# An mLSTM cell and a squared-ReLU FFN on one core: output gates by Tanh, and another order around chunk 2

## Chip, cores, metric

The kernel runs on one core of one Trainium2 chip. The metric is the device time of one execution in microseconds (us); where several executions are given, their median counts. A profile is of one execution. TensorE (PE), VectorE (DVE), ScalarE (ACT), GpSimd (POOL) and SyncE (SP, which here only issues DMAs) each work off their own instructions in the order of the program; semaphores hold an instruction until what it needs is there.

## What is computed

There are 4 batches, 8 heads, 768 steps and a head dimension of 40. The attention part is a recurrence with exponential gates; its output is gated, joined over the heads to rows of 320 and sent through a squared-ReLU feed-forward network (FFN) of width 2048. Everything is float32, and the weights come as float64, as word pairs.

```python
m_new = max(f_gate[t] + m, i_gate[t])
f_stab, i_stab = exp(f_gate[t] + m - m_new), exp(i_gate[t] - m_new)
C = f_stab * C + i_stab * outer(v[t], k[t])
n = f_stab * n + i_stab * k[t]
denom = max(abs(n @ q[t]), 1.0)
o = 1.0 / (1.0 + exp(-o_gate[t]))
y[t] = o * (C @ q[t]) / denom
...
x = y as rows of (batch, step), 320 wide           # 3072 rows
out = max(x @ w_in, 0.0) ** 2 @ w_out
```

## The kernel before

**Tiling.** The 3072 rows are 24 chunks of 128 steps (`NT`), six to a batch; two chunks make a group of the FFN (`GT`). Within a chunk the recurrence is a masked product: `transposes` turns keys and queries, `scores(s)` multiplies them on TensorE (L535), `weigh(s)` makes the decay weights W with exponentials on ScalarE (L464, L468; `mask` on GpSimd at L422 comes first), `weighted(s)` multiplies scores and W on VectorE to P (L549), and `attend(s)` forms three products: `hi` from the state C carried over (L558), `dC` for the new state (L565) and `hp` from P (L572). GpSimd updates the state (L586, L591). `normalise(s)` (from L730) divides by the clipped denominator, multiplies by the output gate `og` and makes the row tile x; `turn_rows(s)` turns it by TensorE (L774) and ScalarE copies it into xT (L775), the input of the first FFN products `ffn1(g, pp)` (L796, L807). Their results go through `relu_half` (L820) and `square_half` (L826) on ScalarE. From chunk 6 (`X_SQ`) on, `normalise_turned` (from L708) takes the place of `normalise`, and x is turned through memory.

**Weights.** The float64 weights arrive in 18 pieces. For each, `Rounding.words` makes two tiles, mag and low, on ScalarE (L211, L213), and `Rounding.join` puts them together: three VectorE operations (L222, L226, L227) and an add on GpSimd (L231), which also lets the next piece be fetched. `rounding.step()` is one of each, with the words a piece ahead of the join. ffn1(0,0) needs pieces 0 to 2; ffn1(0,1) pieces 3 and 4; ffn1(0,2) pieces 5 to 7; ffn1(0,3) pieces 8 and 9.

**Order.** The order is written out by hand and no scheduler moves it. An opening (L1069 to L1128) runs chunks 0 and 1 and prepares chunk 2; a loop of eight steps u (L1133 to L1185) takes chunks 2 to 5, two steps to a chunk, each with one `ffn1`; the long loop over `parts` (L1213) takes chunks 6 to 23, with the FFN products mixed in. In the long loop the attention work is spread over four places `at` per chunk.

**Buffers that matter here.** PSUM gives attention three banks in turn (`ps_at`): scores take two, and the next `hi`, `dC` and `hp` take the third and then the two of the scores once `weighted` has read them. FFN products take banks of `ps_h`: three in the opening, so the second bank of one `ffn1` is the first of the one before, free when its ReLU has read it.

**Gates.** `load_o` brings the output gates, and `sigmoid(s)` (L381) puts them through ScalarE's Sigmoid, in place, 128x320 a chunk. It is called for chunks 0 and 1 before attend(0), for 2 and 3 in the opening, for 4 to 7 at u = 5, and for four chunks at a time in the long loop (L1273). ScalarE's functions come from tables, and a load (ACT_TABLE_LOAD) stands ahead of the first sigmoid of each place and ahead of the first exponential after it (L464 in the opening and the loop of eight, L445 later). On ScalarE the opening runs, after the exponentials of chunk 1: gates 0 and 1, words of pieces 2 and 3, xT of chunk 0, key and query copies of chunk 2, gates 2 and 3, xT of chunk 1, exponentials of chunk 2, words of pieces 4 and 5, exponentials of chunk 3.

Of the kernel before, what the change touches and what calls it, by code (L numbers as in the profile page):

```python
# [13 lines left out]
AF = mybir.ActivationFunctionType  # L14
ALU = mybir.AluOpType
# [14 lines left out]
def kernel(  # L30
# [27 lines left out]
    nc = tc.nc  # L58
    B, H, S, D = q.shape
# [187 lines left out]
    rounding = Rounding()  # L247
# [37 lines left out]
    st = {}  # L285
# [14 lines left out]
    KQ_SQ, X_SQ, ROT = 7, 6, 8  # L300
# [76 lines left out]
        og = st.setdefault(s, {})["og"] = st["og", r][:, s - s0]  # L377
        nc.sync.dma_start(og, o_gate[b, :, c * P : (c + 1) * P, :].rearrange("h p d -> p h d"))

    def sigmoid(s):  # L380
        nc.scalar.activation(st[s]["og"], st[s]["og"], AF.Sigmoid)  # L381

    def load_A(s):
        b, c = divmod(s, NB)
# [154 lines left out]
    def weighted(s):  # L539
        d = st[s]  # L540
        d["P"] = []
        for i in range(2):
            heads = slice(i, H, 2)
            t = d["W"][:, heads, :] if s < ROT else d["W"][:, i::2, DP:]
            if s < W_IN:
                at = 2 * H * P + W * (2 * (s % 2) + i)
                t = flat_c[:, at : at + W].rearrange("p (j t) -> p j t", j=PR)
            d["P"].append(t)
            nc.vector.tensor_tensor(t, d["sc"][i], d["W"][:, heads, :] if s < ROT else t, op=ALU.mult)  # L549
# [180 lines left out]
    def normalise(s):  # L730
        d = st[s]
        num = d["num"]
        if num is not d["hp"]:
            nc.vector.tensor_tensor(num[:], num[:], d["hp"][:], op=ALU.add)
        dm = work.tile([P, H], F32, name="dm")
        nc.vector.tensor_scalar(dm[:], num[:, :, D], scalar1=-1.0, scalar2=1.0, op0=ALU.mult, op1=ALU.max)
        nc.vector.tensor_tensor(dm[:], dm[:], num[:, :, D], op=ALU.max)
        nc.vector.reciprocal(dm[:], dm[:])

        x = d["x"] = work.tile([P, 3 * P], F32, name="x_sb")  # L740
        x3 = x[:, :DM].rearrange("p (h d) -> p h d", d=D)
        nc.vector.tensor_tensor(x3, num[:, :, :D], d["og"], op=ALU.mult)
        nc.vector.tensor_tensor(x3, x3, dm[:].unsqueeze(2).to_broadcast([P, H, D]), op=ALU.mult)
        nc.vector.tensor_copy(x[:, DM:], x[:, DM - KR : DM])

# [23 lines left out]
    def turn_rows(s):  # L769
        d = st[s]  # L770
        t = xT_half(s)
        tp = ps_at.tile([P, 3, P], F32, name="tp", tag="at")
        for a in range(3):
            nc.tensor.transpose(tp[:, a, :], d["x"][:, a * P : (a + 1) * P], ident[:])  # L774
        nc.scalar.copy(t, tp[:])  # L775
        del st[s]
# [329 lines left out]
    load_A(2)  # L1106
    load_o(2)
    load_o(3)
    sigmoid(0)
    sigmoid(1)  # L1110
    attend(0)
    rounding.step()
    normalise(0)
# [7 lines left out]
    idle(4)  # L1121
    transposes(2)
    idle(4)
    sigmoid(2)
    sigmoid(3)
    turn_rows(1)
    weigh(2, masked=True)
    rounding.step()  # L1128


# [2 lines left out]
    for u in range(8):  # L1133
        s = 2 + u // 2
        relu_half()
        if u % 2 == 0:
            if u == 0:
                ffn1(0, 0)
                scores(s)
                rounding.step()  # L1140
            else:
                turn_rows(s - 1)
                scores(s)
                ffn1(u // 4, u % 4)
            if u == 2:
                rounding.words()
            weighted(s)
            if u == 2:
                mask(s + 1)
                rounding.join()  # L1150
                rounding.join()
                weigh(s + 1, masked=True)
                rounding.words()
            else:
                weigh(s + 1)
                square_half()
        else:
            load_A(s + 2)
            for r in {1: (4,), 3: (5, 6), 5: (7,), 7: ()}[u]:
                load(r)  # L1160
            if u == 5:
                for r in range(4, 8):
                    sigmoid(r)
            attend(s)
            if u == 3:
                square_half()
            rounding.join()
            normalise(s)
            for r in {5: (8,), 7: (9,)}.get(u, ()):
                load(r)  # L1170
            for r in {5: (7,), 7: (8,)}.get(u, ()):
                pair_up(r)
            if u > 4:
                load_o(2 * s)
                load_o(2 * s + 1)
            transposes(s + 1)
            rounding.words()
            ffn1(u // 4, u % 4)
            square_half()
        if u < 4:  # L1180
            load_o(4 + u)
        while rounding.done < NEXT[u]:
            rounding.step()
        if u in WIN_SUMS:
            sums_of_win(WIN_SUMS[u])  # L1185
# [27 lines left out]
    for n, (which, g, i) in enumerate(parts):  # L1213
        s, at = 6 + n // 4, n % 4
        if n == 5:
            brought.close()
            late = ctx.enter_context(tc.tile_pool(name="late", bufs=1, side="right"))
        even = s >= 8 and s % 2 == 0
        fast = which == 1
        if at == 0:  # L1220
            if s < 8 or even:
                do(scores, s)
            if even:
                do(turn_kq, s + 1)
            if s < 8 or even:
                do(weighted, s)
        if at == 1:
            do(attend_begin, s)
            if even:
                do(lambda s: scores(s, ("h", "h")), s + 1)  # L1230
            if fast:
                ffn1_rows(g, 0, True)
            do(attend_end, s)
            do(decays, s + 1)
            do(mask, s + 1)
            if n > 4 and not even and not fast:
                do(turn_kq, s + 1)
            do(decay_C, s + 1)
            if s > X_SQ and not fast and not even:
                do(turn_squares, s - 1)  # L1240
            do(store_num, s)
            do(load_num, s)
            do(load_squares, s + 2)
            if even:
                do(load_A, s + 2)
        if 5 <= n < 8:
            sums_of_weights(n - 5)
        if n == 6:
            sums(1, slice(0, NPAIR), (1, 2))
        if n == 8:  # L1250
            sums_of_weights(3)
            sums(1, slice(0, NPAIR), (3,))
        if n == 9:
            sums(1, slice(0, NPAIR), (4,))
        if which == 2 and i == 3 and g == NG - 2:
            sums(g + 1, slice(0, NPAIR), (2,))
        if which == 2 and g > 1 and i < 2:
            sums(g, slice(0, NPAIR), (3 + i,))
        if n == 0:
            ffn1_begin(g)  # L1260
            sums_of_x(g)
            sums_of_win(2)
        if at == 3 and s >= 8 and s % 2 == 0 and s // 2 - 1 < NG:
            sums_of_x(s // 2 - 1)
        if at == 2 and not fast:
            if even:
                do(turn_squares, s - 1)
            if n > 4:
                do(scale_q, s + 1)
        if at == 3:  # L1270
            if s % 4 == 3:
                for r in range(s + 1, min(s + 5, NT)):
                    sigmoid(r)  # L1273
        if fast:
            if i % 2:
                ffn1_close(g, i // 2, i == 1)
                if at == 1 and g > 2:
                    do(turn_kq, s + 1)
                    do(turn_squares, s - 1)
            else:  # L1280
                ffn1_open(g, i // 2)
                if i == 0 and g > 2:
                    sums(g - 1, slice(0, NPAIR), (2,))
            if at == 2 and g > 2:
                do(scale_q, s + 1)
        elif g == 0:
            ffn2(g, *divmod(i, 2))
        else:
            ffn2_fast(g, i)
        if at == 2:  # L1290
            do(lambda s: weigh(s, masked=True), s + 1)
            ffn1_square()
            if n < 4:
                do(turn_kq, s + 1)
                do(scale_q, s + 1)
            if even:
                do(weighted, s + 1)
            do(normalise_turned, s)
            do(store_rows, s)
            if not even:  # L1300
                do(load_A, s + 2)
            if s > 6:
                do(load_o, s + 5)
            do(load_rows, s)
            if s == 6:
                do(pair_up, s + 3)
        if s > 6 and at == (3 if even else 2):
            do(pair_up, s + 3)
        if s > 6 and at == 3:
            if s == 7:  # L1310
                load(s + 3)
            do(load, s + 4)
        if n in (9, 25):
            spread_slots(2 + n // 25)
        if at == 0:
            ffn1_square()
        if n < 5:
            while rounding.done < LAST[n]:
                rounding.step()
# [30 lines left out]
```

## Time and profile before

| what | value |
|---|---|
| median of 6 executions | 502.83 us (499.59 to 509.69) |
| the executions | 499.59, 500.57, 502.09, 503.56, 504.05, 509.69 us |
| the profiled execution | 503.56 us; span 501.7 us, mean granted TensorE clock 0.993 |
| TensorE busy by stretch | 20 to 32 us: 10.39; 32 to 45: 11.92; 45 to 60: 14.38; 60 to 75: 13.26; 75 to 90: 15.00 |
| VectorE busy, the same stretches | 10.56; 10.88; 14.01; 9.26; 11.62 |
| ScalarE busy, the same stretches | 7.86; 9.52; 13.35; 9.98; 12.19 |
| TensorE busy, 150 to 450 us | 299.6 of 300 us |
| exponentials of a chunk, L464 | 389 ns each at 128x128, eight together 2.45 us |
| sigmoid, L381 | 454 ns each at 128x320 by itself, four together 1.55 us |
| table loads | 13, 1283 ns each: 6 at L381, 4 at L445, 2 at L464, 1 at the start |

The busy time of an engine says how full it is in a stretch, not that it sets the pace there; where the last engine to be ready changes from step to step, the chain of waits shows it. "Granted clock" is the share of full speed that the throttle let TensorE have. Matmul ends are modelled, and spans on GpSimd are rough. Shifts in VectorE rows of one and the same shape, such as 0.43 and 1.40 us for L226 at 128x512, come with GpSimd work that runs at the same time.

### The profile page before, as it was taken

To read this page: it belongs to the slowest core of one execution; us is meant where nothing else is said; L and a number is where in the kernel's file an instruction comes from. 1 tells how busy PE (TensorE), PEld (TensorE's weight loads), DVE (VectorE), ACT (ScalarE), POOL (GpSimd) and SP (SyncE) were. 2 spreads that over 40 slices of the span, in tenths; PEclk is the share of its full clock that TensorE was granted. 3 is DMA by queue.
4 is the path that set the end of the run, shared out by engine and by line. 5 is a ranking of instruction groups with operands and counts; after the bars stand their busy time and mean duration, and the time that the engine had idled before them with its cause. 6 is when DMAs were issued, how large, how long until landed. Compare 5 with 4: busy or idle time off the path is not lost.

```text
span 501.7 us, 15218 instructions
## 1 busy us (share of the span) xinstructions
PE 490.4 (98%) x6168; PEld 455.7 (91%) x6169; DVE 345.0 (69%) x700; ACT 249.4 (50%) x524; POOL 221.0 (44%) x317
## 2 busy tenths in 40 slices
PE   9989989999999999999999999999999999999997
PEld 4867868888689999999999999999999999999997
DVE  8588957868877676786777677667866856735441
ACT  3867857955632462393453581551681550423400
POOL 3346732352289457358557458449435031020000
PEclk9999979999999999999999999999999999999999
DMA  9999895854596696597687587578666532200000
GB/s 185 220 225 213 239 217 105 219 91 106 121 182 131 159 180 144 138 180 160 135 163 168 115 164 183 122 148 179 137 132 137 109 96 59 75 14 14 4 26 28
DMA packets 196167, 68.02 MB, mean 136 GB/s; under 512 B 158704, under 2 KB 186064, under 8 KB 196096
## 3 DMA queue, kind: packets, MB, share of 16 engines
q1 hardware_dynamic: 190560, 57.50, 55.7%
q0 software_dynamic: 5440, 9.34, 8.0%
q8 instruction: 49, 0.80, 0.7%
q10 hardware_dynamic: 96, 0.20, 0.1%
q14 instruction: 22, 0.18, 0.1%
HBM read 54.71 MB, written 18.01 MB: 145 GB/s over the span
## 4 chain that ended last, share of the span: by engine, by line
PE 80%; DVE 8%; DMA 4%; ACT 3%; SPq 2%; issue 2%; POOL 0%; DVEq 0%; POOLq 0%; ACTq 0%
PE h_ps L887 32%; PE h_ps L963 21%; PE h_ps L1012 6%; PE h_ps L796 3%; PE h_ps L833 3%; PE numT L652 2%; DMA kqT<-kq_rows 2%; PE numT L633 2%; PE hp L572 1%; DMA num_rows<-tn 1%; PE idle L1056 1%; PE numT L663 1%; DVE mag L226 1%; SPq L703 1%; PE tp L535 1%
## 5 line engine op out<-in xcount | busy, mean ns | idle before, releaser
L887 PE MATMUL h_ps<-T,S 128*128 128x160 f32 x352 | 51.4, 299 | 0.0
L993 ACT COPY r_sb<-h_ps 128x512 f32<-128x512 f32 x18 | 10.5, 585 | 81.7 <-PE h_ps L963 81.7
L887 PE MATMUL h_ps<-w_out,g 128*128 128x160 f32 x336 | 49.2, 303 | 0.0
L887 PEld LDWEIGHTS h_ps<-T,S 128*128 128x128 f32 x352 | 49.0, 190 | 0.0
L428 POOL TENSOR_SCALAR_AFFINE_SELECT A_bc<-A_bc 64x512 f32<-64x512 f32 x32 | 26.0, 812 | 51.9 <-ACT kq L445 45.7
L887 PEld LDWEIGHTS h_ps<-w_out,g 128*128 128x128 f32 x336 | 46.1, 190 | 1.3 <-issue 0.7
L903 DVE TENSOR_TENSOR y_sb<-y_sb,h_ps 128x160 f32<-128x160 f32 x44 | 14.1, 320 | 47.8 <-PE h_ps L887 47.8
L963 PE MATMUL h_ps<-xT,w_in 128*128 128x128 f32 x320 | 43.0, 278 | 0.8 <-ACT r_sb L976 0.8
L963 PE MATMUL h_ps<-lent_t,w_in 128*128 128x128 f32 x320 | 42.2, 275 | 0.0
L963 PEld LDWEIGHTS h_ps<-xT,w_in 128*128 128x128 f32 x320 | 38.9, 192 | 2.4 <-issue 1.0
L1012 PE MATMUL h_ps<-xT,w_in 64*64 64x128 f32 x960 | 39.1, 272 | 0.0
L963 PEld LDWEIGHTS h_ps<-lent_t,w_in 128*128 128x128 f32 x320 | 38.9, 192 | 0.2 <-issue 0.2
L963 PE MATMUL h_ps<-lent_t 128*128 128x128 f32 x320 | 39.0, 275 | 0.0
L963 PEld LDWEIGHTS h_ps<-lent_t 128*128 128x128 f32 x320 | 37.3, 192 | 0.0
L458 ACT ACTIVATE A_bc<-A_bc,b_R 128x64 f32<-128x64 f32 (+1 forms) x128 | 35.7, 362 | 2.9 <-POOL A_bc L428 2.5
L1012 PEld LDWEIGHTS h_ps<-xT,w_in 64*64 64x64 f32 x960 | 34.8, 133 | 1.3
L340 POOL DMA_DIRECT2D va<-in_v_dram x56 | 34.3, 621 | 2.9 <-DMA va<-in_v_dram 1.4
L683 DVE STREAM_TRANSPOSE tn<-numT 128x256 f32<-128x256 f32 x36 | 14.0, 428 | 28.7 <-PE numT L633 19.7
L796 PE MATMUL h_ps<-xT,w_in 128*128 128x256 f32 x128 | 32.1, 407 | 1.2 <-POOL w_in L231 0.6
L478 POOL TENSOR_TENSOR vw<-va,A_bc 128x328 f32<-128x328 f32 x13 | 10.3, 796 | 50.8 <-ACT A_bc L458 50.7
L796 PEld LDWEIGHTS h_ps<-xT,w_in 128*128 128x128 f32 x128 | 25.4, 204 | 5.8 <-POOL w_in L231 1.0
L955 POOL TENSOR_TENSOR lent_t<-xT 128x128 f32<-128x128 f32 (+1 forms) x18 | 12.5, 713 | 36.3 <-DVE xT L766 36.3
(202 smaller groups left out, 1194.5 us busy)
## 6 DMA issues: line engine op xcount, KB each, us to landing
A_bc<-a_slots SPq DMA_DIRECT2D x32, 256.0 KB, 5.0
num_rows<-tn SPq DMA_DIRECT2D x18, 256.0 KB, 2.4
kq<-num_rows SPq DMA_DIRECT2D x72, 64.0 KB, 2.0
raw<-in_moe_w_out_dram SPq DMA_DIRECT2D x7, 640.0 KB, 4.6
kqT<-kq_rows SPq DMA_DIRECT2D x34, 128.0 KB, 3.0
og<-in_o_gate_dram SPq DMA_DIRECT2D x24, 160.0 KB, 5.3
out_dram<-y_sb SPq DMA_DIRECT2D x24, 160.0 KB, 3.1
raw<-in_moe_w_in_dram SPq DMA_DIRECT2D x7, 512.0 KB, 5.6
```

The costliest lines, as they stand in the source:

```text
L340: eng.dma_start(dst[HALVES[n], PR * (1 - late_keys) : PR * (2 - late_keys)], src[HALVES[late_keys], PR * m : PR * (m + 1)],)
L428: nc.gpsimd.affine_select(part, part, compare_op=ALU.is_ge, fill=-1e30, base=0, pattern=[[0, PR], [0, 2], [1, DP]], channel_multiplier=-1,)
L458: nc.scalar.activation(A[0][:, x, to], A[0][:, x, to], AF.Exp, bias=b_R[:, b, c, own, x : x + 1],)
L683: nc.vector.transpose(to[:, 2 * m : 2 * m + 2], d["numT"][m].rearrange("p c t -> p (c t)"))
L796: nc.tensor.matmul(hs[i][:, n, :], lhsT=w_in[:, a, fb * P : (fb + 1) * P], rhs=xT[:, :, a, :], start=(n == 0 and a == 0), stop=False,)
L833: nc.tensor.matmul(o_ps, lhsT=st["g2", g][:, fb, j * P : (j + 1) * P], rhs=w_out[:, fb, :], start=(fb == 0), stop=(fb == NF - 1),)
L887: nc.tensor.matmul(to, lhsT=lhsT[:, p], rhs=rhs[:, p, :], start=(start and p == 0), stop=(p == NPAIR - 1), skip_group_check=True,)
L903: add = lambda to, a, b: nc.vector.tensor_tensor(to, a, b, op=ALU.add)
L955: sub = lambda to, a, b: eng.tensor_tensor(to, a, b, op=ALU.subtract)
L963: nc.tensor.matmul(to[:, n, :], lhsT=lhsT[:, 4 * q + n, :], rhs=rhs, start=(start and n == 0), stop=True, skip_group_check=True,)
L993: nc.scalar.copy(m1[:], X[:])
L1012: nc.tensor.matmul(to[cols, n, :], lhsT=w_in2[rows, 4 * q + n, cols], rhs=rhs, start=(start and n == 0), stop=True, skip_group_check=True,)
```

## The change

It has two parts.

The gates: sigmoid(o) is written as 0.5 + 0.5 tanh(o/2). `half_tanh(s)` takes the place of `sigmoid(s)`; for chunks 0 to 5 only the Tanh is done there, and the rest goes into `normalise`: the denominator is doubled, and the product num * og becomes (og + 1) * num. For chunks 6 to 23 a second pass, a Copy with scale and bias 0.5, finishes the gate, and `normalise_turned` is as before.

The order: scores(2) move from behind ffn1(0,0) to the end of the opening, ahead of weigh(2); the gates of chunks 2 and 3 move behind weigh(2); and at u = 0 the rounding step (the words of piece 5, the join of piece 4) moves from ahead of weighted(2) to behind it.

```diff
-    def sigmoid(s):
-        nc.scalar.activation(st[s]["og"], st[s]["og"], AF.Sigmoid)
+    def half_tanh(s):
+        og = st[s]["og"]
+        nc.scalar.activation(og, og, AF.Tanh, scale=0.5)
+        if s >= X_SQ:
+            nc.scalar.activation(og, og, AF.Copy, bias=0.5, scale=0.5)
...
-        nc.vector.tensor_scalar(dm[:], num[:, :, D], scalar1=-1.0, scalar2=1.0, op0=ALU.mult, op1=ALU.max)
-        nc.vector.tensor_tensor(dm[:], dm[:], num[:, :, D], op=ALU.max)
+        nc.vector.tensor_scalar(dm[:], num[:, :, D], scalar1=-2.0, scalar2=2.0, op0=ALU.mult, op1=ALU.max)
+        nc.vector.scalar_tensor_tensor(dm[:], in0=num[:, :, D], scalar=2.0, in1=dm[:], op0=ALU.mult, op1=ALU.max)
...
-        nc.vector.tensor_tensor(x3, num[:, :, :D], d["og"], op=ALU.mult)
+        nc.vector.scalar_tensor_tensor(x3, in0=d["og"], scalar=1.0, in1=num[:, :, :D], op0=ALU.add, op1=ALU.mult)
...
     idle(4)
-    sigmoid(2)
-    sigmoid(3)
     turn_rows(1)
+    scores(2)
     weigh(2, masked=True)
+    half_tanh(2)
+    half_tanh(3)
     rounding.step()
...
             if u == 0:
                 ffn1(0, 0)
-                scores(s)
-                rounding.step()
             else:
...
             weighted(s)
+            if u == 0:
+                rounding.step()
```

The other calls of `sigmoid` (chunks 0 and 1, u = 5, the long loop) become calls of `half_tanh` in the same places.

More of the change, by code (lines that the diff above doesn't have):

```diff
@@ L1108 @@
     load_o(3)
-    sigmoid(0)
-    sigmoid(1)
+    half_tanh(0)
+    half_tanh(1)
     attend(0)
@@ L1162 @@
                 for r in range(4, 8):
-                    sigmoid(r)
+                    half_tanh(r)
             attend(s)
@@ L1272 @@
                 for r in range(s + 1, min(s + 5, NT)):
-                    sigmoid(r)
+                    half_tanh(r)
         if fast:
```

## The prediction

> **What bounds the kernel now.** I read the page first, then the waits of TensorE by stretch, then the chain that ended last.
>
> ```profile
> PE 490.4 (98%) x6168; PEld 455.7 (91%) x6169; DVE 345.0 (69%) x700; ACT 249.4 (50%) x524; POOL 221.0 (44%) x317
> ```
>
> TensorE stands still for only 501.7 - 490.4 = 11.3 us, tail included. Busy time by stretch puts 0.9 us of that into 104 to 150 us and 0.4 us into 150 to 450 us, so nothing ScalarE saves there can shorten the run by more than that. The rest is in the opening. These are TensorE's waits between 20 and 104 us:
>
> ```profile
> PE tp L774 <- ACT g L820: 1.2, 1, 1.2
> PE dC L565 <- DVE g_c L549: 1.1, 1, 1.1
> PE tp L774 <- DVE x_sb L743: 1.0, 1, 1.0
> PE h_ps L963 <- ACT r_sb L976: 0.8, 1, 0.8
> PE h_ps L796 <- POOL w_in L231: 0.6, 1, 0.6
> PE h_ps L796 <- ACT xT L775: 0.6, 1, 0.6
> PE tp L774 <- DVE x_sb L744: 0.6, 1, 0.6
> ```
>
> Seven waits, 5.9 us; the first and last stand together, ahead of turn_rows(3). From there (66.8 us) TensorE runs nearly gapless to the end, so the run ends earlier by what that point moves. The chain up to it, 26 to 68 us (start, length, what):
>
> ```profile
> 31.98 1.28 ACT L464
> 35.83 0.57 ACT mag L211
> 36.49 0.44 DVE mag L222
> 36.95 1.40 DVE mag L226
> 38.37 0.70 DVE mag L227
> 40.43 1.10 POOL A_bc L422
> 65.43 1.04 DVE x_sb L744
> ```
>
> It runs: a table load, the exponentials of weigh(2), the words of piece 4, its join on VectorE and GpSimd, the mask of chunk 3, the exponentials of chunk 3, ScalarE's work behind them (ReLU of the first products, key copies, words of piece 6), then VectorE's joins until x(3). So the opening is paced by ScalarE, VectorE and GpSimd in turn; TensorE's small waits are its slack.
>
> **Part 1: the gates.** Of the 13 table loads (six at L381, four at L445, two at L464, one at the start) one is left in the instruction order of the changed kernel. The row of the six:
>
> ```profile
> L381 ACT ACT_TABLE_LOAD x6 | 7.7, 1283 | 0.1
> ```
>
> 12 x 1.283 = 15.4 us of ScalarE go. Here the Trainium skill ("ScalarE: Activation LUTs", section "What ACT_TABLE_LOAD costs") asks for more: 1283 ns plus a drain of about 1380 ns, 2.66 us a switch, by which 12 would free 32 us and the one in the chain 2.66. The trace shows no drain: the copy ahead of the load ends at 31.96, the load starts at 31.98 and the first exponential at 33.27. I take 1.28.
>
> Added: a Copy for each of chunks 6 to 23, 18. The trace has no such pass over 128x320 in SBUF; the nearest row is the sigmoid, four back to back in 1.55 us, 0.39 each: 18 x 0.39 = 7.0 us. Tanh itself is taken at the sigmoid's time; between two functions of one shape nothing in the trace shows a difference. Net ScalarE -8.4 us, mostly worth nothing.
>
> Where it is worth nothing: for each later group of four chunks (8 to 11, and so on) the block at L381 goes from 1.28 + 1.55 = 2.83 to 8 x 0.39 = 3.10, 0.27 longer. Behind it wait the ReLU L1029 (at 218.04 without a gap) and then the copy L907, ahead of which ScalarE idles 0.90, 0.77 and 0.77 us for TensorE; that covers it. Without the cover it would be 0.27 x 3 = 0.8 us. At chunks 8 to 11 the idle behind is 3.07 us. The other load of each group, ahead of the decays L445, goes under a TensorE that does not wait. In u = 5 the 2.83 become six passes (2.33), and the load at 86.57 goes while TensorE is busy: nothing.
>
> normalise (six times): two of its operations become scalar_tensor_tensor. Row for that form: 0.69 us at 128x512 (L227); the multiply of now takes 0.44 at 128x320, the two-input L549 0.68 at 128x512. Element cost is alike, so +0.01 by the one comparison, and by L227 scaled (0.69 x 320/512 = 0.43) nothing. I allow 0.05 each; at most two lie in the chain (x(2), x(3)): +0.1. Both forms read two SBUF inputs, as before, and those wait for GpSimd as before (L737 took 1.47 us beside a 1.53 us add).
>
> **Part 2: order in the opening.** In the new order, scores(2) sit ahead of ffn1(0,0) on TensorE; on VectorE the two products of P(2) stand ahead of the join of piece 4; on ScalarE the gates of chunks 2 and 3 come behind weigh(2). No DMA is issued elsewhere in SP's or POOL's order.
>
> ScalarE: xT(1) ends at 31.96 as now, the exponentials run 31.98 to 34.43 (2.45) and dec to 34.63, two gates to 35.46 (0.83), the words of piece 4 give mag at 36.1 (now 36.39). The load's 1.28 are thus mostly spent again on gates ahead of piece 4's words: what moves is 0.45 at most there.
>
> TensorE: scores(2), 1.06 us, go into the 0.57 us in which it now waits for xT(1); ffn1(0,0) starts at about 32.5 (now 32.01) and hi(2) at 37.2 (now 37.62). dC(2) needs the bank that the first product of P(2) frees.
>
> VectorE: the join of piece 3 ends at 35.05 as now; P(2) takes 2 x 0.65 to 36.35 instead of 38.98 to 40.27. So dC(2)'s 1.07 us go. The join of piece 4 starts at 36.35 instead of 36.49. The next question is its shift, L226: 1.40 us there, 0.43 where nothing else holds the port. The add of piece 3 on GpSimd ran 36.50 to 38.05 beside it. In the new order vw(2) follows the exponentials (34.5 to 35.25), and piece 3's add runs 35.25 to 36.5, beside P(2), which reads PSUM and SBUF and in no row is slowed (L549 679 to 693 ns in all 14). So the shift runs free, and the join ends at 36.5 + 0.43 + 0.43 + 0.69, about 38.1 instead of 39.07: 0.95 earlier. If the add collides after all, the join ends at about 39.0: 0.1. These are the two ends; I take the first, because the add's start is fixed by a join that does not move.
>
> What is late next: mask(3) ends at about 40.55 (41.52), the exponentials of chunk 3 start 0.95 earlier. TensorE, 1.5 us ahead by then, reaches the second bank of ffn1(0,1) at 43.6 and waits 0.2 for the ReLU behind those exponentials; then ffn1(0,2) waits 0.8 to 1.4 for piece 6 (0.6 now). So its gain is cut back to the chain's: 0.95 - 0.1 = **0.85 us** at x(3), and from 66.8 on it stays.
>
> Sum: 503.56 (span 501.7 and 1.86 around it) - 0.85 = 502.7. This execution lies 0.73 above the median of its six, so on the median: 502.0.
>
> **The clock.** It decides more than the edit. Two stretches, 60 to 67 and 67 to 74 us (PE, PEld, DVE, ACT, POOL busy; then granted clock, DMA):
>
> ```profile
> 60.00:67.00 7.00, 5.26 (x29) 3.82 (x29) 6.25 (x9) 4.88 (x9) 5.25 (x5) 1.00 1.28 244
> 67.00:74.00 7.00, 7.00 (x29) 5.76 (x28) 3.01 (x5) 5.11 (x13) 2.03 (x2) 0.52 1.29 221
> ```
>
> The clock fell to 0.50 at 67.0 and came back at 73.6. The price: scores(4) (L535, 66.77 to 68.66) 1.89 us instead of 1.10 (48.48 to 49.58), ffn1(1,0) 6.16 instead of 3.55 (59.68 to 63.23): 3.4 us. Without it this execution would be at 500.2, and two of the six are at 499.6 and 500.6. The skill ("TensorE: Matmul & The Clock Gate", "What's actually happening") tells of a free-running window of 3413 ns and a throttle after an idle window: the half clock did last two such windows, but no window was idle. There were 1.18 + 0.56 = 1.74 us of waiting within 2.2. By the page's rule neither kernel could lose clock here; by the row it does where a window holds that whole stretch, by an estimate from the page's window (3.41 - 2.15)/3.41, over a third of executions. 1.57 us within 2.1 (29.9 to 32.0) did not do it. The new order does not shorten the stretch: both sides of it move.
>
> **Rivals.**
> - Half clock goes: x(3) catches up with TensorE by 0.1 to 0.2 us, or windows fall otherwise in most executions. 503.56 - 0.85 - 3.4 = 499.3. For: the threshold lies between 1.57 and 1.74. Against: TensorE gains at least as much as x(3), so the gap should grow.
> - Slower: a second half clock. The new waits at 43.6 and 48.5 (0.2 and up to 1.4) lie in TensorE's way where it now waits 0.6; if piece 4's join collides, they grow, and the gap ahead of turn_rows(3) reaches 2 us. Above about 1.7 us in a window it costs 3.4: 503.56 - 0.1 + 3.4 = 506.9, and 505 if in half the executions. Against: the two lie 5 us apart.
> - Nothing moves: the collision eats the gain, 503.5; on the median 502.7. For: the gates of chunks 2 and 3, now out of the chain, take the load's place in it. Against: VectorE's order, not ScalarE's, sets the join.
> - It does not do what it says: if Tanh needed another table, two loads a group would stay and only Copies be added. The single load in the order excludes it.
>
> **Numbers.** Forecast 0.50; half clock gone 0.24; slower 0.13; nothing 0.13. Range: low 503.56 - 1.4 (chain and port at their best) - 3.4 = 498.8; high 505.0. Against the 502.83 of now, 0.5% (about what can be told from no change) is 2.5 us: faster 0.26, within 0.60, slower 0.14.
>
> **What would show it.** One table load; P(2) ending near 36.4; L226 of piece 4 at 0.43; mask(3) near 39.5 to 40.6; no wait of dC on L549; a new wait of ffn1(0,1) or (0,2); x(3) near 65.6. Wrong it would be if words of piece 4 came no earlier, if the clock row differs, or if L1029's block delays TensorE.

## The result, and the profile after

Over 72 executions the median of before is 500.5 us (the six known ahead lie high), and that of the changed kernel over 35 is 499.68 us (496.86 to 504.81). The ratio is 0.9993, interval 0.9976 to 1.001: no difference that this comparison can tell, as forecast. Two further comparisons of the same pair, on other chips, gave 0.9973 [0.9947, 1.0] and 0.9981 [0.9949, 1.0013], so the three estimates put the change at 0.4 to 1.4 us, and none of them is clear of no change. (Ratios leave out disturbed executions, those over 1.5% above the fastest; medians and clock counts below do not, so that a ratio is not the quotient of two medians.)

The profiled execution of the changed kernel took 496.86 us, at a span of 495.1. That is its fastest execution, and its distance to before's profile (6.6 us of span) is not the effect of the change. Lines behind the edits have moved by 3: L774 is now L777, L796 is L799, L549 is L552, L422 is L425.

The engines' busy time, from the page, and TensorE's waits from 20 to 104 us (line waiting, releaser, us in total, times, longest):

```profile
PE 485.8 (98%) x6168; PEld 452.2 (91%) x6169; DVE 345.3 (70%) x700; ACT 241.3 (49%) x530; POOL 223.6 (45%) x317
```

```profile
PE tp L777 <- ACT g L823: 1.2, 1, 1.2
PE tp L777 <- DVE x_sb L746: 1.1, 1, 1.1
PE h_ps L799 <- POOL w_in L231: 1.0, 1, 1.0
PE h_ps L966 <- ACT r_sb L979: 0.8, 1, 0.8
PE h_ps L799 <- ACT g L823: 0.6, 1, 0.6
```

TensorE's own work has shrunk by 4.6 us (490.4 to 485.8) although it executes the same 6168 matmuls: most of that is the clock, as the stretches below show. Of the waits, dC's 1.1, the 0.6 for xT and the 0.6 for x(3) are gone; of the two of ffn1 (L799) one is new (0.6) and one longer (1.0 for 0.6). The sum is 4.7 us for 5.9.

The chain of waits, 26 to 68 us (start, length, what):

```profile
34.79 0.78 DVE g_c L552 x2
...
35.99 1.02 DVE mag L222
37.04 0.44 DVE mag L226
37.50 0.70 DVE mag L227
...
39.55 1.35 POOL A_bc L425
...
50.32 3.29 PE h_ps L799 x14
```

No table load and no ScalarE step stands ahead of P(2) any more; VectorE leads from 31.7 us up to the mask. P(2) (L552) goes first, the shift L226 takes 0.44 instead of 1.40, and the add of piece 3, now at 35.44 to 36.71, blocks the operation in front of it instead: L222 takes 1.02 for 0.44. The mask takes 1.35 for 1.10, beside a VectorE shift of the next piece that is held for 1.20.

The stretches that the prediction showed (PE, PEld, DVE, ACT, POOL busy; granted clock; DMA):

```profile
60.00:67.00 7.00, 5.84 (x42) 4.51 (x41) 5.24 (x10) 5.44 (x11) 4.67 (x4) 1.00 1.28 232
67.00:74.00 7.00, 7.00 (x48) 5.96 (x48) 3.77 (x8) 6.70 (x16) 2.27 (x3) 1.00 1.17 220
```

The clock stays at 1.00 from 67 to 74 us, where it was 0.52. In these 7 us TensorE issues 48 matmuls for 29.

Where the 6.6 us came from, at markers common to both traces: turn_rows(1) begins 0.19 earlier before any edit on the path has acted (30.89, 30.70); 0.43 are gained from there to the exponentials of chunk 3 (41.55 to 40.93, less the 0.19); 0.8 because the copy ahead of turn_rows(3) takes 0.20 us for 1.03 (in before a GpSimd mask began 0.11 us ahead of it, here 0.25 after it); 3.4 is the half clock (0.50 for 6.8 us); the rest, 1.8 us, arises behind 75 us, where single executions of one kernel differ by as much (shown below).

### The profile page after: what moved, and what is told of

The parts are those of the page before. It is cut to its first block, busy times and chain, and to the rows that moved or that the text cites. A ratio compares the mean times of both kernels' runs of the same rounds, so it can differ in the third digit from the quotient of the medians.

```text
span 495.1 us, 15226 instructions
## 1 busy us (share of the span) xinstructions
PE 485.8 (98%) x6168; PEld 452.2 (91%) x6169; DVE 345.3 (70%) x700; ACT 241.3 (49%) x530; POOL 223.6 (45%) x317
## 4 chain that ended last, share of the span: by engine, by line
PE 91%; ACT 2%; SPq 2%; DVE 2%; DMA 1%; issue 1%; POOL 1%; POOLq 0%; DVEq 0%; ACTq 0%
PE h_ps L890 35%; PE h_ps L966 25%; PE h_ps L1015 7%; PE h_ps L799 4%; PE h_ps L836 4%; PE numT L655 3%; PE numT L636 2%; PE numT L666 1%; PE h_ps L810 1%; PE idle L1059 1%; PE tp L530 1%; PE h_ps L530 1%; SPq L318 1%; PE hp L575 1%; DMA kq<-in_q_dram 1%
## 5 line engine op out<-in xcount | busy, mean ns | idle before, releaser
L431 POOL TENSOR_SCALAR_AFFINE_SELECT A_bc<-A_bc 64x512 f32<-64x512 f32 x32 | 24.6, 768 | 47.4 <-ACT kq L448 41.0
L966 PEld LDWEIGHTS h_ps<-xT,w_in 128*128 128x128 f32 x320 | 38.9, 192 | 2.4 <-issue 1.0
L799 PE MATMUL h_ps<-xT,w_in 128*128 128x256 f32 x128 | 29.9, 384 | 1.7 <-POOL w_in L231 1.0
L799 PEld LDWEIGHTS h_ps<-xT,w_in 128*128 128x128 f32 x128 | 23.5, 190 | 5.8 <-POOL w_in L231 1.4
```

Source lines behind the costliest of these rows:

```text
L431: nc.gpsimd.affine_select(part, part, compare_op=ALU.is_ge, fill=-1e30, base=0, pattern=[[0, PR], [0, 2], [1, DP]], channel_multiplier=-1,)
L799: nc.tensor.matmul(hs[i][:, n, :], lhsT=w_in[:, a, fb * P : (fb + 1) * P], rhs=xT[:, :, a, :], start=(n == 0 and a == 0), stop=False,)
L966: nc.tensor.matmul(to[:, n, :], lhsT=lhsT[:, 4 * q + n, :], rhs=rhs, start=(start and n == 0), stop=True, skip_group_check=True,)
```

## The experiments

The prediction left two things to be settled: which part moves the chain, and what halves the clock. The expectations call the theories by letters: A and B are about what moves the chain (the load that goes, the order), C and D about the clock (C: the wait ahead of turn_rows(3) halves it; D, formed after the first four runs: the wait of dC(2) does, in the midst of short products).

All results, grouped by chip. "Full clock" counts executions whose mean granted clock is 0.9985 or more; "lost" is 500 us x (1 - mean granted clock), averaged over the executions.

| kernel | median, us | ratio to before | full clock | lost, us |
|---|---|---|---|---|
| before, chip 1 | 501.31 | 1 | 3 of 67 | 3.8 |
| gates alone | 499.35 | 0.9977 [0.995, 1.0005] | 16 of 22 | 0.8 |
| order alone | 500.50 | 0.9997 [0.9965, 1.0029] | 10 of 14 | 0.8 |
| changed + 5 idle ahead of turn_rows(3) | 500.70 | 0.9982 [0.9954, 1.001] | 13 of 22 | 1.4 |
| before + 5 idle ahead of turn_rows(3) | 501.93 | 1.0009 [0.9986, 1.0031] | 4 of 22 | 2.9 |
| before, chip 2 | 503.71 | 1 | 1 of 63 | 4.4 |
| changed, again | 501.95 | 0.9973 [0.9947, 1.0] | 8 of 22 | 1.8 |
| before + 5 idle ahead of dC(2) | 502.62 | 0.9984 [0.9957, 1.001] | 7 of 22 | 1.9 |
| gates alone + idle at both | 500.05 | 0.9948 [0.9923, 0.9973] | 9 of 10 | 0.3 |
| changed, heavy gates | 503.12 | 0.9993 [0.9969, 1.0017] | 12 of 20 | 1.1 |
| before, chip 3 | 500.90 | 1 | 4 of 51 | 3.5 |
| changed + idle in three waits | 499.39 | 0.9956 [0.993, 0.9981] | 18 of 22 | 0.6 |
| gates alone + idle at both, again | 499.08 | 0.9981 [0.9957, 1.0004] | 16 of 22 | 0.6 |
| changed, once more | 499.88 | 0.9981 [0.9949, 1.0013] | 8 of 14 | 0.8 |
| before, chip 4 | 501.36 | 1 | 0 of 20 | 3.9 |
| before + idle at both | 498.77 | 0.9961 [0.9931, 0.9991] | 10 of 14 | 0.6 |

In the comparison of the result itself the changed kernel had the full clock in 19 of 36 executions. Medians of different chips are not compared.

### The gates alone, the order alone

```diff
 # gates alone: the changed kernel with the order of before
     idle(4)
+    half_tanh(2)
+    half_tanh(3)
     turn_rows(1)
-    scores(2)
     weigh(2, masked=True)
-    half_tanh(2)
-    half_tanh(3)
...
                 ffn1(0, 0)
+                scores(s)
+                rounding.step()
...
             weighted(s)
-            if u == 0:
-                rounding.step()
```

> The gates part alone, the old order. Counted from the start of turn_rows(1) on TensorE, the exponentials of chunk 3 begin at +10.7 us before and +10.2 after, and x(3) is multiplied out at +34.5 and +34.1. Theory A (the table load sat in the chain, and the order spends part of it): with the gates alone the words of piece 4 come 1.1 us earlier, the exponentials of chunk 3 begin at +9.4 to +9.7 and x(3) at +33.2 to +33.6, earlier than in both. Theory B (the order is what gains, the gates nothing): +10.6 and +34.4, as before. The median within 0.3% of before in either case; the trace decides.

```diff
 # order alone: before (Sigmoid, 13 loads, gates 2 and 3 where they were)
     turn_rows(1)
+    scores(2)
     weigh(2, masked=True)
...
                 ffn1(0, 0)
-                scores(s)
-                rounding.step()
...
             weighted(s)
+            if u == 0:
+                rounding.step()
```

> The new order alone, with Sigmoid, and the gates of chunks 2 and 3 where they were, so all 13 loads stay. Theory A: P(2) now stands ahead of piece 4's join while the exponentials still end 1.3 us later, so the join ends later than before: exponentials of chunk 3 at +10.9 to +11.2, x(3) at +34.7 to +35.0, a median 0 to 0.1% above before. Theory B: +10.2 and +34.1 as in the changed kernel.

The expectations count from the start of turn_rows(1). That start moves by over 1 us between executions (29.76, 30.84, 30.89, 30.70 for gates alone, order alone, before, changed), for a reason that lies ahead of the edits around chunk 2. In the profile of the gates alone GpSimd's mask of chunk 2, which waits for its DMA, begins at 28.03 (27.20 in before). The state update behind it then runs beside other VectorE operations than in before: the operations that are held stand behind the start of turn_rows(1), not ahead of it. VectorE's rows of before, then those of the gates alone with one GpSimd row:

```profile
30.86 0.20 DVE L744 COPY x_sb<-x_sb 128x64 f32<-128x64 f32 x1
31.43 0.43 DVE L226 TENSOR_SCALAR lent_t<-lent_t 128x512 int32<-128x512 int32 x1
32.49 0.42 DVE L222 TENSOR_SCALAR mag<-mag 128x512 f32<-128x512 f32 x1
...
36.49 0.43 DVE L222 TENSOR_SCALAR mag<-mag 128x512 f32<-128x512 f32 x1 [1.44 <-ACT mag L211]
```

```profile
29.74 0.61 DVE L747 COPY x_sb<-x_sb 128x64 f32<-128x64 f32 x1
30.72 0.98 DVE L226 TENSOR_SCALAR lent_t<-lent_t 128x512 int32<-128x512 int32 x1
32.34 0.42 DVE L222 TENSOR_SCALAR mag<-mag 128x512 f32<-128x512 f32 x1
...
35.25 0.41 DVE L222 TENSOR_SCALAR mag<-mag 128x512 f32<-128x512 f32 x1
```

```profile
30.38 1.04 POOL L594 TENSOR_TENSOR C_sb<-C_sb,Cd 128x328 f32<-128x328 f32 x1
```

The third row of each, where piece 3's join begins (32.49, 32.34, 32.45 and 32.31 in the four kernels), lies behind the held operations and is the better origin:

| start, us after piece 3's join begins | before | gates alone | order alone | changed |
|---|---|---|---|---|
| mask(3) | 7.94 | 6.83 | 8.13 | 7.24 |
| exponentials of chunk 3 | 9.06 | 7.96 | 9.45 | 8.62 |
| last copy of x(3) | 32.94 | 31.83 | 33.37 | 32.53 |

The runs further down that differ from these kernels only in places that do not touch this part of the chain repeat it: the exponentials come at 9.05 to 9.41 in three more profiles of before, at 7.95 and 8.08 in two more of the gates alone, at 8.50 to 8.62 in five more of the changed kernel.

So the gates by themselves move the chain by 1.0 to 1.1 us, the order by itself delays it by 0.4, and the two together gain 0.4 to 0.6. This is Theory A, and B falls. In the expectations' own count the order alone lies where A has it (11.06 and, at x(3), 34.98). The gates alone miss it in the first profile (10.54, from a start that came early) and meet it in the one where x(1)'s copy and the shift behind it are not held (9.69, second run of "gates alone with both waits filled"). The medians cannot tell the parts apart: the intervals of both ratios reach past 1.

VectorE's rows around P(2), first gates alone, then order alone (start, length, line, tiles):

```profile
35.70 1.38 DVE L226 TENSOR_SCALAR mag<-mag 128x512 int32<-128x512 int32 x1
37.11 0.69 DVE L227 SCALAR_TENSOR_TENSOR mag<-raw,mag 128x512 int32<-128x512 int32 x1
37.72 1.28 DVE L552 TENSOR_TENSOR g_c<-tp,g_c 128x512 f32<-128x512 f32 x2
```

```profile
35.42 1.29 DVE L549 TENSOR_TENSOR g_c<-tp,g_c 128x512 f32<-128x512 f32 x2 [0.41 <-ACT g_c L464]
36.63 1.40 DVE L222 TENSOR_SCALAR mag<-mag 128x512 f32<-128x512 f32 x1
```

With the gates alone the join of piece 4 no longer waits for its words and starts 2.91 us after that of piece 3 (4.00 in before). Its shift is held for 1.38 by the add of piece 3 (35.41 to 36.80), as it was in before. With the order alone the load is still there; P(2) waits for the exponentials and starts 0.6 later than in the changed kernel, the join starts 4.18 after piece 3's, and the add (36.46 to 37.74) meets L222 at its start: 1.40. With both, P(2) starts at 34.79 and covers the first half of that add, so that the shift is free and L222 loses 0.58; but P(2) stands ahead of the join, which starts 3.68 after piece 3's. The order thus takes back 0.5 to 0.7 us of the chain that the gates gain. What it brings is a dC(2) without a wait (0.52 with the gates alone).

### Idle products ahead of turn_rows(3)

```diff
 # in the changed kernel, and (second run) in before
             else:
+                if u == 4:
+                    idle(5)
                 turn_rows(s - 1)
```

> The changed kernel with five more idle products of zeros ahead of turn_rows(3), where TensorE waits 1.2 to 1.7 us. Theory C (that wait is what sometimes halves TensorE's clock for 3.4 to 6.8 us): the mean granted clock is 0.998 or more in every execution but the odd one, against 0.992 to 0.997 in 16 of 36 of the changed kernel; the median falls by 0.5 to 1.5 us against it, to about 0.2% below before. Rival: the half clock comes from other waits (8 to 50 us) or from none that the program sets: the shares of clocks stay as they are, and the time too.

> The same five idle products in the kernel before. Theory C: clock 0.998 or more in nearly all executions, the median 0.5 to 1.5 us (0.1 to 0.3%) below before, and the same as the changed kernel with them but for 0.4 us. Rival: no change of clock or time.

The products fill the wait that the prediction held for the cause: TensorE has no wait from 60 to 70 us in the changed kernel with them. The full clock did not follow, 13 of 22 against 19 of 36 without them (in the comparison of the result), and 4 of 22 against 3 of 67 in before. Theory C falls as the main cause. A small share is not excluded: before loses 2.9 us of clock with these products and 3.8 without. The profile of before with them shows the half clock elsewhere. First TensorE's rows, then the stretch from there (columns as above):

```profile
37.10 1.12 PE L558 MATMUL hi<-C_sb,kqT 128*128 128x82 f32 x8
39.48 1.09 PE L565 MATMUL dC<-vw,kq 128*128 128x82 f32 x8 [1.26 <-DVE g_c L549]
40.41 3.03 PE L572 MATMUL hp<-va,g_c 128*128 128x41 f32 x16
```

```profile
41.00:47.70 6.70, 6.70 (x27) 6.16 (x27) 5.72 (x10) 6.46 (x16) 4.00 (x5) 0.50 1.30 229
```

The clock is at 0.50 in all of this stretch, which begins 1.5 us after a wait of 1.26: hp takes 3.03 us for its usual 1.92. What stands ahead of it is one wait among products of 82 and 41 columns. In the changed kernel that wait is gone. It is gone too with the order alone and down to 0.5 us with the gates alone, and both of these lose 0.8 us of clock where before loses 3.8. From this Theory D was formed.

### Idle products ahead of dC(2)

```diff
 # before, in attend(s) between hi and dC; into a bank of ps_o, not read
+        if s == 2:
+            fill(5)        # five bf16 products, 128x512
```

> The kernel before, with five idle products of zeros between hi(2) and dC(2), where TensorE waits 1.1 to 1.3 us; nothing else moves. Theory D: full clock in half or more of the executions instead of a few per cent, and a mean 1 to 2 us below before, like the changed kernel. Rival: the shares stay as they are, as they did with the same filling ahead of turn_rows(3).

> The changed kernel once more, beside the kernel before on one chip, with every execution's clock. Theory D (the wait of dC on P(2) ahead of the products of attend(2), which load many weights and stream few columns, is what halves the clock in the kernel before; the new order takes it away): full clock (0.9985 or more) in about half of its executions against under a tenth before, mean time 1 to 2 us below before, median 0.5 to 1.5 us below. Rival (chance, or the chip): equal shares of full clock, equal means.

```profile
39.64 1.12 PE L558 MATMUL hi<-C_sb,kqT 128*128 128x82 f32 x8
40.59 1.25 PE L1065 MATMUL fill<-zeros 128*128 128x512 bf16 x5
41.68 1.01 PE L567 MATMUL dC<-vw,kq 128*128 128x82 f32 x8
```

TensorE's rows show the five products in 1.25 us and no wait ahead of dC. Nothing else of before is touched, and its lost clock falls from 4.4 to 1.9 us, about the changed kernel's 1.8 on the same chip; full clock 7 of 22 against 1 of 63. That this wait is where most of the clock is lost is shown: full clock in half of the executions, as D expected, was missed, but the lost clock fell by more than half. Whether the waiting itself does it or too little work in this stretch is not shown, since the products change both. It is not the only place: 15 of the 22 executions still lose some clock, and in this run's own profile the half clock stands at 33.2 to 36.6 us, behind the two waits around turn_rows(1) (1.14 and 0.57 us). The time follows only in part: ratio 0.9984 [0.9957, 1.001].

The unaltered changed kernel ran beside it. It had the full clock in 8 of 22 executions, where about half was expected. Its profile has the full clock (1.0) as the one under the result has, yet a span of 499.3 us for 495.1. TensorE's waits of that profile behind 104 us:

```profile
PE numT L636 <- DVE A_bc L552: 1.8, 2, 1.4
PE numT L666 <- DVE kq L628: 0.4, 2, 0.3
PE numT L655 <- DVE A_bc L552: 0.3, 1, 0.3
```

These are 2.5 us; the profile shown under the result has a single wait of 0.3 there. One kernel, the full clock in both: over 2 us between two executions come from waits for VectorE's P in the long loop. A difference of that size between two profiles says nothing of an edit.

### Gates alone with both waits filled

The kernel "gates alone" with two `fill` products ahead of dC(2) and two ahead of turn_rows(3).

> The gates alone in the old order, with two idle products in the wait of dC(2) and two ahead of turn_rows(3). Theory D: full clock in three quarters of the executions or more (0.73 without the filling), median 499 to 499.5, 0.3 to 0.5% below before, the fastest of all. Rival: as the gates alone, or slower by the 0.9 us of the filling.

> Gates by tanh in the old order, two idle products in dC(2)'s wait and two ahead of turn_rows(3), as before on another chip. If its gain is real it repeats: ratio to before 0.993 to 0.997, full clock in three quarters or more of the executions, and at least 0.7 us below the changed kernel beside it. If it was that chip or that hour, it lies within 0.4 us of the changed kernel.

On chip 2 it was faster than before beyond the interval (0.9948) with the full clock in 9 of 10; on chip 3 the ratio was 0.9981 [0.9957, 1.0004] with 16 of 22, its median 0.8 us under the changed kernel's. The intervals overlap. The expected ratio of 0.993 to 0.997 was missed on chip 3. The share of full clock repeats, but the gates alone had 16 of 22 without idle products (chip 1), so that the products add anything here is not shown, and a lead over the changed kernel is not shown either.

### Heavier gates in the long loop

```diff
             nc.scalar.activation(og, og, AF.Copy, bias=0.5, scale=0.5)
+            for _ in range(2):
+                nc.scalar.activation(og, og, AF.Copy, bias=0.0, scale=1.0)
```

> The changed kernel with two more Copies over each gate of chunks 6 to 23 (scale 1, bias 0). The block ahead of L1032 in the last three groups grows from 3.45 to about 6.9 us. Theory (ScalarE's cover there is nearly used up: 0.3 us are left of 0.9): TensorE waits some 2 to 3 us in each of three groups for a bank, 6 to 9 us in all, 1.2 to 1.8% slower. Rival (the gates of the long loop are far from the path): no change.

ScalarE's rows at the end of a gate block, the changed kernel and then the heavy one:

```profile
208.77 0.46 ACT L382 ACTIVATE og<-og 128x320 f32<-128x320 f32 x1
209.25 0.47 ACT L384 ACTIVATE og<-og 128x320 f32<-128x320 f32 x1
...
212.22 0.58 ACT L1032 ACTIVATE g<-h_ps 128x512 f32<-128x512 f32 x1
213.10 0.29 ACT L910 COPY y_sb<-h_ps 128x160 f32<-128x160 f32 x1 [0.30 <-PE h_ps L890]
```

```profile
217.49 0.97 ACT L386 ACTIVATE og<-og 128x320 f32<-128x320 f32 x2
218.37 0.58 ACT L1034 ACTIVATE g<-h_ps 128x512 f32<-128x512 f32 x1
218.84 0.28 ACT L912 COPY y_sb<-h_ps 128x160 f32<-128x160 f32 x1
```

The block grew from 3.45 to 7.5 us, and the idle time ahead of the copy (0.90 in before, 0.30 in the changed kernel) is used up. Still no wait of TensorE on ScalarE appears behind 104 us, and the median is 1.2 us over the changed kernel's, not 6 to 9: this expectation was missed. TensorE's waits on VectorE come to 4.6 us there (2.5 and 0.3 in two profiles of the changed kernel); whether the heavier gates lengthen them is not shown. The idle time ahead of the next instruction is only the first layer of the cover; that the banks of PSUM and g behind it hold the rest is likely, not tested. So the 0.6 us by which a block has grown against before costs nothing that could be seen.

### The remaining waits of the changed kernel, and before with both waits filled

```diff
 # changed kernel; fill as above
 # between the halves of ffn1(0, 1)
+            if g == 0 and pp == 1 and i == 1:
+                fill(3)
 # in the wait of ffn1(0, 2)
+                    if g == 0 and pp == 2 and i == n == 0 and a == 1:
+                        fill(4)
 # ahead of turn_rows(3)
+                if u == 4:
+                    fill(5)
```

> The changed kernel with idle products in PE's remaining waits before 65 us: three between the halves of ffn1(0, 1), four in the wait of ffn1(0, 2), five ahead of turn_rows(3); the block's results are not read. If the half clock is started by idle time of PE inside the short-product stretch (Theory D, carried from dC(2)'s wait to these waits), the full clock is granted in three quarters or more of the executions (about half did for the changed kernel without them) and the median is 0.5 to 1.5 us below the changed kernel's of the same chip. If what is left of the half clock in the changed kernel comes from the products of attend(2) and turn_rows(2), which now stand in one row without a wait, the share stays at a third to a half and the time within 0.5 us of the changed kernel's.

> The changed kernel unaltered, as the reference for the two beside it. Ratio to before 0.996 to 1.000, full clock in a third to a half of the executions.

The share of full clock is 18 of 22, as D has it, against 8 of 14 beside it, a difference that chance could still make; the median is 0.49 us lower, at the edge of what was expected. With the interval 0.993 to 0.9981 this kernel is faster than before. It is not separated from the changed kernel.

```diff
 # before: Sigmoid and order untouched
+        if s == 2:
+            fill(4)        # in attend, ahead of dC
...
+                if u == 4:
+                    fill(5)        # ahead of turn_rows(3)
```

> The kernel before, Sigmoid and old order, with four idle products in dC(2)'s wait and five ahead of turn_rows(3); their results are not read. It takes the clock out of the comparison of before and changed. If the two waits are what halves the clock (Theory D, both waits), the full clock is granted in half or more of the executions. Then, if the edits themselves save the 0.4 us that the two traces show at x(3) and TensorE keeps it, this kernel stays 0.4 us or more above the changed kernel with its waits filled: ratio to before 0.996 to 0.999. If the edits are worth nothing or cost something once the clock is full (what the executions at full clock, 498.6 of before against 499.4 of changed on the last chip, hint at), it does as well as that kernel or better: ratio 0.993 to 0.996.

Full clock in 10 of 14 (before beside it: 0 of 20), and a ratio of 0.9961, within 0.0005 of the changed kernel with its waits filled (0.9956). The figure is on the border between the two expectations. What it does show: nine idle products put into the kernel before, with none of the change's edits, bring as much as the change, as far as these comparisons can tell. By these two ratios, from different chips, the edits' own worth with the clock out of the way is 0 within about 2 us. Against the 7 of 22 with dC(2)'s wait alone filled (chip 2), the 10 of 14 also speak for a share of the wait ahead of turn_rows(3).

The profile of this run lost clock where neither wait is. First the 5 us ahead and the half clock (columns as above), then TensorE's rows:

```profile
9.25:14.25 5.00, 4.97 (x34) 3.22 (x32) 4.21 (x6) 1.64 (x4) 0.51 (x1) 1.00 1.21 191
14.30:17.65 3.35, 3.35 (x10) 1.98 (x10) 1.46 (x3) 3.00 (x12) 1.45 (x2) 0.50 1.12 158
```

```profile
12.40 1.15 PE L412 MATMUL A_ps<-A_sb,sel 32*128 32x128 f32 x8
13.39 0.50 PE L278 MATMUL tp<-ident,i_sb 32*128 32x32 f32 x6
13.73 0.54 PE L278 MATMUL tp<-ident,A_sb 32*128 32x32 f32 x6
14.20 1.95 PE L501 MATMUL tp<-ident,kq 128*128 128x128 f32 x8
```

TensorE had no wait there. So a wait is not needed for a half clock; here it followed products of 32 rows and 32 or 128 columns. In before's profile the same products passed at full clock.

## Why the prediction held, and where it did not

**The forecast of no measurable change** held, and its 0.85 us is near what three comparisons give (0.4 to 1.4 us). That the size fits is luck: the chain gave half of what was put, and the clock, which the sum left as it was, came back in most executions. One reading of the profile was loose: of the 11.3 us in which TensorE stands still, 3.2 lie in the tail behind 450 us, not in the opening.

**The gates.** Right: 12 loads of 1283 ns gone, no drain behind the one in the chain; ScalarE's busy time fell by 8.1 us for the 8.4 of the sum; the multiply (0.44 at 128x320) and the comparison (0.17 at 128x8) cost nothing more as scalar_tensor_tensor, for the 0.05 each that were allowed. Mis-sized: a pass of the gate block at 0.39. A Copy starts 0.48 after the Tanh whose result it needs, the next Tanh 0.38 after the Copy; eight passes took 3.45 us, 0.43 each, where 3.10 was put. The cover took it, and the heavy gates show that it would have taken more. The sum did not price the gates apart from the order; by themselves they bring 1.0 to 1.1 us at the exponentials of chunk 3.

**The order, up to the join.** Right: P(2) ends at 36.07 (36.35), the shift runs in 0.44 (0.43), the join ends at 38.19 (38.1), no wait of dC. The step "So the shift runs free" held but left out what the add blocks in its place: L222, 0.58 us. A start 0.36 earlier than put (35.99 for 36.35; 0.18 of it stood already at piece 3's join) made up for part of it. Against the gates alone the order is a loss of 0.5 to 0.7 us on the chain, where the sum had it as the source of the gain.

**From the join to x(3).** "the exponentials of chunk 3 start 0.95 earlier" failed: 0.43, measured from turn_rows(1) (0.44 from piece 3's join). Two terms were mis-sized: L222, and the mask at 1.35 for 1.10. The two waits came where forecast, ffn1(0,1) with 0.6 (0.2) and ffn1(0,2) with 1.0 (0.8 to 1.4). At x(3) 1.4 us were gained in this pair of profiles, but 0.8 of it by the copy that missed a GpSimd mask by 0.25 us; the sum had no term for that. "from 66.8 on it stays" is not borne out by anything: two profiles of the changed kernel differ by over 2 us in waits behind that point.

**The clock.** This is the step that failed: "The new order does not shorten the stretch: both sides of it move", with the stretch ahead of turn_rows(3) as cause. The runs put the main place 26 us earlier, into dC(2)'s wait, which the sum itself had cancelled: filled alone, it took the lost clock from 4.4 to 1.9 us; the stretch ahead of turn_rows(3), filled alone, from 3.8 to 2.9. The prediction looked only at the half clock of its one profile. "Half clock goes" stood among its rivals, at 3.4 us. That rival is half right: 3.0 and 2.3 us less of clock are lost on the two chips where both kernels were counted (in the executions that the ratios count), but by another cause than it named, and the time fell by 1.4 and 0.9 us only. Its threshold, between 1.57 and 1.74 us of waiting, is not borne out: half clocks also began with a single wait of 1.26 in the 5 us ahead (before with idle products), with one of 0.52 (gates alone) and with none (before with both waits filled). The Trainium skill ("TensorE: Matmul & The Clock Gate", "What's actually happening") asks for an idle window ahead of a throttle. No window without work stands ahead of the half clocks shown; one began after a wait of 1.26 us among short products, one after 5 us in which TensorE was busy for 4.97.

**The other rivals.** A second half clock did not come, the new waits of 0.6 and 1.0 us notwithstanding. That Tanh needs a table of its own is excluded by the single load. "Nothing moves" is wrong for the chain (0.43 us) and can't be told from the truth by the time.

**Open.** In before, an execution that loses 1 us more of clock is 0.7 to 0.85 us longer (a straight line through the executions that the ratios count, four chips). By this the 3.0 and 2.3 us of clock that the changed kernel wins should have brought about 2 us; they brought 1.4 and 0.9, with intervals up to 2.6. The shortfall is not clear of the noise. If it is real, either the edits cost something at full clock, or a TensorE that is earlier waits again for P in the long loop, as one of its profiles shows (2.5 us). Before with both waits filled (2.8 us of clock won, 1.9 us of time, interval 0.5 to 3.5) does not decide it.

## What to carry to other kernels

Where one profile shows a half clock, collect the granted clock of many executions before naming its cause: the place differs from one execution to the next, and one wait filled with idle products tells in one run whether it has a part in it. Before two profiles are read from a common marker, see whether the same work runs beside the marker in both. Here a GpSimd mask that came 0.8 us later moved about 1 us of held VectorE work across turn_rows(1); read from there, the 1.1 us that the gates bring look like 0.1. When an edit takes an operation out of a collision, count the blocked operation behind it and what now stands ahead in its queue. And the idle time ahead of an engine's next instruction is the least, not all, of what it can take.

## What the runs showed of the hardware

- The half clock (granted clock 0.50) began at 67.0 us in before, at 41.0 in before with idle products ahead of turn_rows(3), at 33.2 in before with them ahead of dC(2), at 14.25 in before with both waits filled and at 41.2 with the gates alone. It lasted 6.8 us in the first two and 3.4 in the others. In the 5 us ahead of it TensorE had been busy for 3.26, 3.74, 3.29, 4.97 and 4.48 us, while the clock stayed full behind 5 us with 3.93 (36 to 41 us in before) and with 3.84 (60 to 65 us in the changed kernel). The busy share ahead does not tell the two apart.
- Five idle products of 1.25 us together ahead of dC(2) took the share of executions with the full clock from 1 of 63 to 7 of 22; ahead of turn_rows(3), from 3 of 67 to 4 of 22.
- A VectorE operation with two inputs in SBUF, 0.17 us long, took 1.47 beside a GpSimd add, in both forms. The two products with one input in PSUM took the same 1.28 us beside such an add (gates alone, L552 at 37.72, add 37.95 to 39.22) as with GpSimd idle (1.29 at 66.59 in the changed kernel).
